# A local-attention, gated-convolution and MLP kernel: another hand-written list for its first fifth

## The chip, the cores and the metric

The kernel runs as one program on one core of a Trainium2 chip. The core has five engines that run their own instruction queues side by side: TensorE (PE, with its weight loads as PEld), VectorE (DVE), ScalarE (ACT), GpSimd (POOL) and SyncE (SP), which here only issues DMA transfers. The metric is the device time of one execution in microseconds (us), and lower is better.

## The reference

Three layers follow each other, in float32, on a batch of 2, 768 positions, 8 heads of 64:

```python
# 1 attention: each query sees its 31 nearest keys and 24 block summaries
k_sum = k.reshape(B, H, 24, 32, D).max(axis=3)
v_sum = v.reshape(B, H, 24, 32, D).mean(axis=3)
scores_l = where(|i - j| < 16, scale * q @ k.T, -1e9)
scores_s = scale * q @ k_sum.T + log(32)
a = softmax(concat(scores_l, scores_s))
x = a @ concat(v, v_sum)                 # -> (2, 768, 512)
# 2 gated convolution
h = relu(x @ w_in)                       # 512 -> 1024
x = (h * sigmoid(conv3(h, conv_w))) @ w_out
# 3 normalised MLP
x = x + relu(layernorm(x) * g_ln @ w_ch1) @ w_ch2    # 512 -> 2048 -> 512
```

The weights come as 64-bit floats, so the kernel itself narrows them to 32-bit ones, and each factor is split into a high and a low part, so that three fast products make one precise one.

## The kernel before

The kernel describes its work as 1932 numbered pieces (`plan.op`). A piece has a name, the engines that can do it, the pieces that it comes after, and the ring of buffers that it takes a place in. The string `ORDER` lists all of them: `13S 12S 15S` means that piece 13 is traced first, on SP, then 12, then 15. `plan.arrange` reads the list, and each engine's queue holds its own pieces in exactly this order. Nothing is reordered later: an engine that meets a piece whose input is not there stands until it is, and everything behind it in that queue stands too. The same holds for SP: a transfer that has to wait keeps back all transfers listed behind it.

The pieces of the first fifth, with the names used below:

- **Key and query loads** (`lk`, `lq`, L347): six key halves and four query halves of batch 0, 256 KB each, beside three value loads of 512 KB (`lvp`, for the block means). All transfers are on SP's queue.
- **Transposes** of keys and queries (L374): a group of 16 matmuls per half, into PSUM. Each key half is then copied out (`kn`, L265 or L267) and its blocks' maxima are taken (`kmb`, L395, on DVE).
- **The weights** (`lw`, L681 for w_in and L684 for w_out): sixteen loads of 512 KB. Each is narrowed by a DVE piece (L643), an ACT piece (L647) and a DVE piece (L652), then split into a high part (L265 or L267) and a low part (L664, POOL). Six loads have a place; the seventh waits until the first has been split.
- **Pairs** of score tiles. A pair is 128 queries by 8 heads. Its pieces are the mask product M (L479), the scores S (L487, 32 rows of the trace), per half the maximum X (L545, DVE), exponential E (L557, ACT), the sum's reciprocal Q and R, the scaling N (L576), the transpose P (L586) and its copy C; then T (L503), the product of both halves with the values, and the outputs H (high, L265 or L267) and L (low, L529, DVE). T of pair *j* needs two things in its value tile `vw`: the value rows (`lv`, L621) and the 24 rows of block means (`vs`), which `f_vs` puts there either by a DVE copy (L636) or by a DMA on SP (L634).
- **Two warm-up pieces** (L290): `warm0` with ten and `warm` with six products of a zeroed tile with itself, whose result is never read.
- **The convolution layer**: `h` (L741, 12 products in three pieces), then the taps, tanh and gate, and `x` (L818). The first piece of `h`, called h0 below, needs the attention output of pairs 0 to 2: it waits for the halo piece `xh1`, which waits for L of pair 2.

From the end of this first fifth (piece x110, an L818 group that starts at 97.6 us) both lists are the same to the end.

Of the kernel before, what the change touches and what calls it, by code (L numbers as in the profile page):

```python
# [8 lines left out]
115S 187S 57A 210P 197P 240P 239P 241P 214S 228G 104V 229V 88V 89A 211A 111A 198A 230V 215V 221V 165V 222V 110V 242V
231P 183P 2P 212P 249V 406S 243A 97S 250A 223G 244G 224P 188V 112V 106V 245V 251G 90G 116V 246V 232A 185A 247P 117A  # L10
225A 213V 186V 252V 206P 253V 107A 233P 118V 49A 248A 235A 207V 108G 413P 412P 414P 208V 96G 119A 113A 121S 236V 377S
254P 407P 409P 422V 237G 423A 259P 114G 120G 260P 261P 272P 273P 274P 262A 424G 263G 408V 410V 415V 416A 275A 123A 98V
255V 425V 264V 426V 265V 122V 285P 286P 127S 386S 411S 238S 133S 287P 298P 427P 276A 417G 99A 288A 289A 266A 428A 277V
278V 124V 437P 436P 299P 290V 100V 300P 311P 312P 438P 378P 313P 267V 268G 129A 279A 291V 301A 101A 292A 302A 125A
418V 280V 314A 269G 128V 439V 324P 270P 381P 271P 325P 102G 446V 681S 126G 303V 379V 315A 447A 440A 380V 293V 419V
304V 130V 369S 139S 316V 305A 281A 131A 135A 326P 327A 382A 282V 337P 338P 339P 350P 351P 352P 420P 421A 294G 448G
430G 441G 132G 317V 134V 295V 306V 383V 442V 136V 283P 256P 328A 353A 257A 354A 318A 449V 329V 330V 319V 429P 387P
137A 258V 138G 434G 284P 682P 388A 431A 307A 340A 389V 432V 433G 390P 373P 296P 297P 456P 457P 370P 458P 683A 331A
374A 341A 308V 355V 140V 450V 342V 356V 332V 141A 320A 459A 343V 344A 357A 321V 443V 142V 371A 391A 358V 372V 151S
145S 469P 309P 470P 153A 310P 471P 472A 482P 392V 375V 143G 144G 460V 483P 451P 484P 495P 496P 435S 147A 676A 473A  # L20
345V 485A 486A 677A 474V 461V 157S 399S 395S 710S 475V 476A 462V 487V 322P 497P 444P 508P 323P 509P 510P 463A 152V
464V 477V 376V 146V 488V 452A 333A 334V 498A 404A 499A 445A 684P 148V 154V 690P 689P 685A 385V 453P 158V 511A 500V
159A 713P 489A 712P 160V 521P 346A 149A 522P 490V 400V 405A 523P 150G 161A 691P 524A 454A 714P 155A 501V 393S 699V
335P 512A 732S 156G 722V 700A 336P 347V 162G 534P 396V 502A 535P 359A 348P 360G 536P 503V 686G 349P 692V 537A 525G
361P 687S 513V 538A 465G 455V 547P 362A 397S 365P 514V 737S 466V 548P 526V 366A 478G 549P 701V 539V 515A 479G 467P
527V 468P 707G 702V 516V 480P 491A 550A 492V 481P 528A 540V 394V 493P 504A 693A 494P 505G 566P 517G 529V 567P 703V
733P 694V 568P 367V 398V 506P 569A 551A 507P 541A 723A 579P 552V 530G 580P 695V 542V 581P 518V 724G 715V 704P 531G
582A 739P 734A 570V 740P 592P 705A 696V 519P 716A 725V 571V 401V 520P 572V 553V 593P 402A 543G 384V 583A 532P 403S
726G 554A 544V 680A 533P 594P 584V 741P 717V 555V 718V 595A 556G 697P 573A 749V 557G 727P 742V 750A 596G 545P 574V
585V 546P 719V 743A 558P 698V 688S 605P 738S 606P 728A 711S 744G 575G 607P 678G 720P 608A 679G 562P 559A 751G 609G  # L30
586A 735P 576G 761P 610V 706P 736A 563A 587V 760P 721V 618P 759S 588G 752V 619P 745V 753V 762P 597V 904P 770V 620P
598V 577P 621A 611V 560A 771A 622G 631P 708V 589G 632P 709V 633P 599A 772V 578P 600V 763V 754P 634A 601G 612A 905P
623V 729P 764A 773V 746V 624V 906P 774V 625A 730A 747P 907V 755A 590P 602V 908A 731V 644P 635V 645P 626V 591P 765V
613V 914V 646P 614G 766V 636V 603P 647A 748V 775P 767V 604P 776A 637V 915A 657P 627G 658P 659P 768P 660A 778G 628G
926P 638A 756P 769A 639V 561A 909V 910V 927P 777P 757V 911G 758V 928P 779A 615V 916V 917V 912P 929V 616P 648V 930A
780V 617P 649V 781G 629P 650V 661A 640G 936V 630P 651A 931G 662V 937A 782P 564V 663V 932V 783P 641V 933G 913A 784P
796P 785A 642P 786V 652V 797P 653A 664A 654V 798P 938V 939V 787V 810P 799A 788V 811P 800G 665V 789A 812P 924G 940V
# [1424 lines left out]
```

## Time and profile before

| | us |
|---|---|
| median of 3 runs | 473.87 (473.40 to 473.89) |
| the profiled execution | 473.54 |
| its span, first to last instruction | 471.8 |
| PE busy | 461.9 (98%) |
| DVE busy | 352.2 (75%) |
| ACT busy | 249.4 (53%) |
| POOL busy | 142.1 (30%) |

About 1.7 us of the execution lie outside the span. A busy PE is not the whole story: matmuls overlap, and where they run at half the clock they are counted as busy too. DMA is saturated at first (80% and more in the first five of 40 slices) and mostly idle later.

### The profile page before, as it was taken

What the parts mean: (1) busy time and instruction counts of PE and PEld (TensorE: products, weight loads), DVE (VectorE), ACT (ScalarE), POOL (GpSimd) and SP (SyncE); (2) the same over time, 40 slices, a digit from 0 to 9 for tenths busy, and PEclk for the clock granted to TensorE, in tenths of its full rate; (3) what the DMA queues carried; (4) which work ended last, traced back from release to release, by engine and by line L of the source; (5) the groups of instructions that cost most, each with busy time, mean ns of one, the idle gap of its engine ahead of it and who ended that gap; (6) DMA issues with size and microseconds to landing.
All of it is one profiled execution on the core that took longest, in us unless ns stands there. A gap on an engine that the chain in (4) does not pass through costs nothing.

```text
span 471.8 us, 8644 instructions
## 1 busy us (share of the span) xinstructions
PE 461.9 (98%) x3211; PEld 408.6 (87%) x3211; DVE 352.2 (75%) x705; ACT 249.4 (53%) x654; POOL 142.1 (30%) x185
## 2 busy tenths in 40 slices
PE   5999999999999999999999999999999999999996
PEld 5758999888899989988889899999898898998985
DVE  2899999996777857988998874677655677654643
ACT  2788989676766766968954432232343235322010
POOL 3547432554234244232523222131131332002000
PEclk9999999999999999999999999999999999999999
DMA  8999966902002202002221141202222022110213
GB/s 232 327 251 229 246 203 155 176 3 64 1 18 47 92 2 89 1 0 89 92 86 54 39 134 50 86 16 74 89 90 89 3 89 81 44 54 1 99 36 133
DMA packets 56121, 43.26 MB, mean 92 GB/s; under 512 B 34404, under 2 KB 46976, under 8 KB 56080
## 3 DMA queue, kind: packets, MB, share of 16 engines
q1 hardware_dynamic: 55936, 42.65, 32.4%
q8 instruction: 25, 0.41, 0.4%
q14 instruction: 16, 0.13, 0.1%
q10 hardware_dynamic: 144, 0.07, 0.1%
HBM read 39.22 MB, written 3.15 MB: 90 GB/s over the span
## 4 chain that ended last, share of the span: by engine, by line
PE 92%; DVE 3%; DMA 2%; ACT 2%; issue 1%; SPq 0%; POOL 0%; ACTq 0%; DVEq 0%; POOLq 0%
PE acc L1366 26%; PE ch L1288 22%; PE x L818 12%; PE h L741 6%; PE tr L741 5%; PE ch L741 4%; PE tr L487 2%; PE tr L503 2%; PE h L818 2%; PE tr L586 2%; PE tr L367 1%; PE tr L479 1%; PE tr L374 1%; PE x L881 1%; PE x L374 1%; DMA early<-in_k_dram 1%
## 5 line engine op out<-in xcount | busy, mean ns | idle before, releaser
L1366 PE MATMUL acc<-w,cb 128*128 128x512 f32 x570 | 138.1, 390 | 0.0
L1366 PEld LDWEIGHTS acc<-w,cb 128*128 128x128 f32 x570 | 106.4, 188 | 18.4
L1288 PE MATMUL ch<-xb,w 128*128 128x384 f32 x384 | 75.6, 338 | 0.3 <-DVE u L1299 0.3
L1288 PEld LDWEIGHTS ch<-xb,w 128*128 128x128 f32 x384 | 67.8, 188 | 3.2 <-DVE u L1299 1.0
L1299 DVE TENSOR_TENSOR u<-ch,u 128x384 f32<-128x384 f32 x64 | 34.9, 552 | 30.5 <-PE ch L1288 29.8
L1288 PE MATMUL ch<-xt,w 128*128 128x384 f32 x288 | 57.0, 338 | 0.3 <-DVE u L1299 0.2
L771 DVE SCALAR_TENSOR_TENSOR c<-h,ccol,c 128x256 f32<-128x256 f32 (+1 forms) x80 | 48.4, 615 | 9.3 <-POOL c L269 4.9
L1288 PEld LDWEIGHTS ch<-xt,w 128*128 128x128 f32 x288 | 50.8, 188 | 2.8 <-DVE u L1299 1.1
L818 PE MATMUL x<-wo,ghi 128*128 128x512 f32 x160 | 51.1, 401 | 0.0
L1099 POOL TENSOR_TENSOR w<-raw,w 128x512 fp32r<-128x512 f32 (+1 forms) x16 | 20.5, 1283 | 81.9 <-ACT w L1166 75.0
L1308 ACT ACTIVATE cb<-p 128x384 fp32r<-128x384 f32 x32 | 16.5, 519 | 40.4 <-PE acc L1366 23.6
L557 ACT ACTIVATE prob<-tr,nm 128x120 f32<-128x120 f32 x96 | 33.2, 368 | 5.6 <-DVE nm L545 3.6
L647 ACT ACTIVATE raw<-raw 128x512 f32<-128x512 f32 x32 | 21.0, 672 | 26.8 <-DMA raw<-in_moe_w_ch_dram 26.8
L741 PE MATMUL h<-xT,wi 128*128 128x258 f32 x216 | 32.0, 289 | 0.0
L818 PE MATMUL x<-wo,glo 128*128 128x512 f32 x80 | 31.6, 395 | 0.0
L818 PEld LDWEIGHTS x<-wo,ghi 128*128 128x128 f32 x160 | 27.9, 189 | 3.3 <-ACT wo L265 0.2
L1308 ACT ACTIVATE cb<-u 128x384 fp32r<-128x384 f32 x32 | 16.1, 521 | 27.4 <-DVE u L1299 27.3
L741 PEld LDWEIGHTS h<-xT,wi 128*128 128x128 f32 x216 | 29.1, 190 | 1.7 <-ACT h L753 0.2
L741 PE MATMUL tr<-xT,wi 128*128 128x386 f32 (+1 forms) x168 | 29.3, 317 | 0.0
L741 PEld LDWEIGHTS tr<-xT,wi 128*128 128x128 f32 x168 | 26.7, 190 | 1.3 <-issue 0.4
L652 DVE SCALAR_TENSOR_TENSOR raw<-raw 128x512 uint32<-128x512 uint32 x32 | 22.9, 727 | 0.7 <-ACT raw L647 0.2
L786 DVE SCALAR_TENSOR_TENSOR gbuf<-c,h 128x256 f32<-128x256 f32 (+1 forms) x40 | 19.3, 487 | 5.2 <-ACT c L776 5.1
(192 smaller groups left out, 830.0 us busy)
## 6 DMA issues: line engine op xcount, KB each, us to landing
raw<-in_moe_w_ch_dram SPq DMA_DIRECT2D x32, 512.0 KB, 3.6
wst<-in_moe_w_out_dram SPq DMA_DIRECT2D x8, 512.0 KB, 4.8
vw<-in_v_dram SPq DMA_DIRECT2D x20, 192.0 KB, 4.6
wst<-in_moe_w_in_dram SPq DMA_DIRECT2D x5, 512.0 KB, 8.3
s_q<-in_q_dram SPq DMA_DIRECT2D x8, 256.0 KB
early<-in_k_dram SPq DMA_DIRECT2D x6, 256.0 KB, 5.0
x2a<-in_moe_w_in_dram SPq DMA_DIRECT2D x3, 512.0 KB
early<-in_v_dram SPq DMA_DIRECT2D x3, 512.0 KB
```

What stands on the lines that cost most here:

```text
L557: A.activation(out=pr[:, p, :], in_=sc[:, p * NK:(p + 1) * NK], func=AF.Exp, bias=nm[:, p:p + 1], scale=1.0, accum_out=sm[:, p:p + 1])
L647: A.activation(out=f, in_=f, func=AF.Prelu, scale=F64_SCALE, alpha=F64_SIGN)
L652: V.scalar_tensor_tensor(out=most, in0=most, scalar=3, in1=least, op0=ALU.logical_shift_left, op1=ALU.bitwise_or)
L741: T.matmul(live["h", i][:, 0:N + 2], w_[:, c, f * 128:(f + 1) * 128], x_[:, c, 0:N + 2], start=(k_ == 0 and c == 0), stop=(k_ == 2 and c = ...
L771: V.scalar_tensor_tensor(out=ct, in0=ht[:, kk:kk + N], scalar=ccol[:, kk * NF + f:kk * NF + f + 1], in1=ct, op0=ALU.mult, op1=ALU.add)
L786: V.scalar_tensor_tensor(out=gt, in0=ct, scalar=1.0, in1=ht, op0=ALU.add, op1=ALU.mult)
L818: T.matmul(x2ps[g, t], l[:, ts_], r[:, f, :], start=(f == 0 and j == 0), stop=(f == NF - 1 and j == 2))
L1099: lambda e: on[e].tensor_tensor(out=hi()[1], in0=from_(), in1=hi()[0].bitcast(F32), op=ALU.subtract),
L1288: T.matmul(bk[k], l[:, c, :], x_[:, c, :], start=j == 0 and c == 0, stop=j == 2 and c == 1)
L1299: lambda e: V.tensor_tensor(out=temp(to), in0=bk[k], in1=temp(x), op=ALU.add), after,
L1308: A.activation(out=half(0, r, y), in_=temp(src), func=AF.Relu)
L1366: T.matmul(acc[key], ct_[n][l][:, r, 128 * t:128 * t + 128], w2[s][k][:, r], start=first and j == 0, stop=done and j == 5)
```

## The change

Only the string `ORDER` differs; no piece is added, removed or rewritten, and 24 lines fewer hold the string, so a line of the program after has a number lower by 24 (L503 becomes L479). The first 563 pieces are listed in another order, and 56 of them on another engine. The list begins:

```diff
-13S 12S 15S 14S 67S 9S 8G 3G 4G 5G 6G 68V 58V 0V 31P 32A 59A 69A 16S 11S 18S 17S 20S 73S 91S 19S 21S 39P 27P 34P 41V
+3G 0V 7G 2P 16S 15S 13S 42P 39P 43A 40A 12S 31P 44V 4G 163G 6G 33V 14S 45G 27P 41V 28A 29V 5G 34P 36V 17S 11S 24P 32A 25A 35V 30V 18S 67S 52P 53A 69A 73S
```

What moves, by names: eight key and query halves lead SP's queue and the first weight comes ninth, where it was fifth; the six-product warm-up leads PE's queue, and the ten-product one moves from in front of the first block-mean product to a place behind the last of them; the maxima of keys lead DVE's queue; the three copies of the block means into `vw` (L636 on DVE) become transfers on SP (L634 before, L610 after); and the transposes of the fourth query chunk, which stood in front of h0, come behind it.

The first place is the start of DVE's queue. Before, `wst` is the first weight, `craw` the convolution's taps, `warm` the zeroed tile, and `ksum` the maxima of keys:

```order
L643 TENSOR_SCALAR wst<-wst 128x512
L643 TENSOR_SCALAR craw<-craw 24x128
L285 MEMSET warm 128x64
L395 TENSOR_REDUCE ksum<-tr 128x2x8 x2
L652 SCALAR_TENSOR_TENSOR wst<-wst 128x512
L652 SCALAR_TENSOR_TENSOR craw<-craw 24x128
L902 COPY crow<-craw 24x128
L395 TENSOR_REDUCE ksum<-x_179 128x2x8
```

The same place after:

```order
L261 MEMSET warm 128x64
L371 TENSOR_REDUCE ksum<-x_127 128x2x8
L371 TENSOR_REDUCE ksum<-tr 128x2x8 x2
L371 TENSOR_REDUCE ksum<-x_182 128x2x8
L371 TENSOR_REDUCE ksum<-x_199 128x2x8
L243 COPY kw_95<-x_199 128x8x64
L243 COPY kw_94<-kw_94 128x4x3x16 x2
L371 TENSOR_REDUCE ksum<-tr 128x2x8
L619 TENSOR_SCALAR wst<-wst 128x512
```

The maxima now stand in front of the first narrowing, and the taps' pieces are far behind.

The second place is SP's queue from the last w_in load that both lists have there (the eighth place of `wst`) to the last transfer that T of pair 2 needs. Before (`vw0` to `vw2` are the value tiles of pairs 0 to 2, `s_q` a later query chunk):

```order
L954 DMA s_q<-in_q_dram 128x8x64 x2
L681 DMA wst<-in_moe_w_in_dram 128x4x256
L621 DMA vw_99<-in_v_dram 80x8x64
L621 DMA vw_99<-in_v_dram 96x8x64
L684 DMA wst<-in_moe_w_out_dram 128x1024
L621 DMA vw_100<-in_v_dram 96x8x64 x2
L621 DMA vw_101<-in_v_dram 96x8x64 x2
```

After (`vsum` is the tile of block means):

```order
L657 DMA wst<-in_moe_w_in_dram 128x4x256
L597 DMA vw_99<-in_v_dram 80x8x64
L597 DMA vw_99<-in_v_dram 96x8x64
L597 DMA vw_100<-in_v_dram 96x8x64 x2
L930 DMA s_q<-in_q_dram 128x8x64 x2
L610 DMA vw_99<-vsum 24x2x512
L597 DMA vw_101<-in_v_dram 96x8x64 x2
L610 DMA vw_100<-vsum 24x2x512
L828 DMA crow<-in_moe_g_ln_dram 4x128
L660 DMA wst<-in_moe_w_out_dram 128x1024
L657 DMA x2a<-in_moe_w_in_dram 128x4x256
L660 DMA wst<-in_moe_w_out_dram 128x1024
L610 DMA vw_101<-vsum 24x2x512
```

The last row, the block means of pair 2, now stands behind three weight loads; before, the value rows of pair 2 stood behind one of them, and the means came by DVE. (`vw_99`, `vw_100` and `vw_101` are the tiles `vw0`, `vw1` and `vw2`.)

## Rows read from the trace of the kernel before

**Rows 1.** The page's busy line of PE, and what PE waited for.

```profile
PE 461.9 (98%) x3211; PEld 408.6 (87%) x3211; DVE 352.2 (75%) x705; ACT 249.4 (53%) x654; POOL 142.1 (30%) x185
PE tr L374 <- DMA early<-in_k_dram: 4.9, 2, 4.0
PE tr L586 <- DVE prob L576: 0.5, 1, 0.5
```

**Rows 2.** Stretches: length, busy of PE, PEld, DVE, ACT, POOL, clock, DMA share, GB/s.

```profile
4.00:12.30 8.30, 7.42 (x68) 7.02 (x70) 2.96 (x8) 2.05 (x4) 1.63 (x7) 1.00 1.05 281
17.80:34.57 16.77, 16.77 (x196) 9.01 (x195) 15.51 (x37) 14.17 (x59) 8.67 (x13) 1.00 1.05 283
34.57:43.92 9.35, 8.90 (x161) 7.11 (x161) 8.83 (x18) 8.49 (x29) 6.46 (x9) 1.00 1.07 210
43.92:98.28 54.36, 54.36 (x530) 49.23 (x529) 53.32 (x109) 45.04 (x138) 23.47 (x32) 1.00 0.79 186
98.28:471.80 373.52, 368.92 (x2180) 331.61 (x2178) 266.46 (x524) 174.86 (x420) 96.35 (x105) 1.00 0.18 58
```

**Rows 3.** Timeline of PE up to 23 us: start, length, instruction, idle before it.

```profile
3.98 1.98 PE L374 MATMUL tr<-ident,early 128*64 128x128 f32 x16 [3.98 <-DMA early<-in_k_dram]
6.84 1.98 PE L374 MATMUL tr<-ident,early 128*64 128x128 f32 x16 [0.88 <-DMA early<-in_k_dram]
8.60 3.63 PE L374 MATMUL x<-ident,early 128*64 128x128 f32 x32
12.01 2.07 PE L374 MATMUL tr<-ident,early 128*64 128x128 f32 x32
15.66 1.04 PE L374 MATMUL tr<-ident,early 128*64 128x128 f32 x16
16.54 1.31 PE L479 MATMUL tr<-mask_r,mask_l 67*64 67x480 bf16 x6
```

**Rows 4.** Timeline of DVE: its first instruction, and the first maximum of scores.

```profile
9.31 0.43 DVE L643 TENSOR_SCALAR wst<-wst 128x512 uint32<-128x512 uint32 x1 [9.31 <-DMA wst<-in_moe_w_in_dram]
...
18.86 0.66 DVE L545 TENSOR_REDUCE nm<-tr 128x4 f32<-128x480 f32 x1 [0.35 <-PE tr L487]
```

**Rows 5.** Timeline of all engines, 32 to 44 us, the pieces around T and h0.

```profile
32.30 0.68 DVE L636 COPY vw<-vsum 24x1024 f32<-24x1024 f32 x1
34.57 1.15 PE L503 MATMUL tr<-probT,vw 120*64 120x64 f32 x32
35.66 1.47 PE L290 MATMUL h<-warm 128*128 128x512 bf16 x6
36.96 0.60 PE L367 MATMUL tr<-ident,s_q 128*128 128x128 f32 x4
39.00 2.21 PE L503 MATMUL tr<-probT,vw 120*64 120x64 f32 x64
41.15 0.58 PE L479 MATMUL tr<-mask_r,mask_l 67*128 67x480 bf16 x2
41.27 0.59 ACT L265 CAST xT<-tr 128x512 fp32r<-128x512 f32 x1
41.52 1.29 DVE L529 TENSOR_TENSOR xT<-tr,xT 128x512 fp32r<-128x512 f32 x2
43.13 1.04 PE L367 MATMUL tr<-ident,s_q 128*128 128x128 f32 x8
43.26 0.34 POOL L267 CAST xT<-xT 128x8 fp32r<-128x8 f32 x2
43.92 1.69 PE L741 MATMUL h<-xT,wi 128*128 128x258 f32 x12
```

**Rows 6.** DMA moved up to 40.53 us, from 10 to 20 us, and from 34.57 to 40.53 us.

```profile
DMA packets 20150, 10.47 MB, mean 258 GB/s; under 512 B 8212, under 2 KB 20016, under 8 KB 20144
...
DMA packets 4657, 3.17 MB, mean 317 GB/s; under 512 B 130, under 2 KB 4656, under 8 KB 4656
...
DMA packets 4048, 1.06 MB, mean 178 GB/s; under 512 B 4040, under 2 KB 4040, under 8 KB 4046
```

More of the change, by code (lines that the diff above doesn't have):

```diff
@@ L9 @@
[L9 to L13, printed above, removed]
@@ L94 @@
[L94 to L95 removed]
+3G 0V 7G 2P 16S 15S 13S 42P 39P 43A 40A 12S 31P 44V 4G 163G 6G 33V 14S 45G 27P 41V 28A 29V 5G 34P 36V 17S 11S 24P 32A 25A 35V 30V 18S 67S 52P 53A 69A 73S
+21S 9S 79S 19S 26V 50P 47A 68V 190P 167P 51V 70V 8V 74V 46V 38G 48A 71A 75A 20S 166P 168P 72G 176V 177A 22S 169V 170A 103S 171G 189P 191P 76V 54P 199V 200A
+178V 179V 63P 64A 180V 181P 65P 192V 80V 193A 81A 105A 172V 201V 202V 173V 203V 37G 104V 55P 217P 106V 77G 58V 23S 82V 194V 174P 182V 66A 49A 216P 218P
@@ new lines @@
+107A 226V 59A 240P 91S 92V 204P 205V 195V 56P 83A 175A 93A 219V 227A 94V 196V 78G 85S 220A 109S 164S 187S 209S 228V 239P 241P 229V 57A 86V 108G 249V 87A
+88V 84G 197P 198V 95A 165S 184G 230G 221G 96G 222V 242V 214S 188S 250A 60V 110V 223V 1P 111A 231P 251G 10S 243A 115S 97S 244V 183P 185A 252V 89A 232A 121S
+215S 112V 224P 206P 234G 253G 225A 186V 212P 210P 254P 377S 207V 208V 211V 245V 213A 246V 113G 90G 255V 413P 114G 233P 235A 412P 117A 236V 414P 61P 247P
+237V 248A 259P 260P 261P 272P 116V 62V 118V 273P 274P 119A 262A 422V 423A 275A 285P 286P 120G 98V 287P 415V 416A 298P 299P 300P 417G 311P 263V 436P 312P
@@ new lines @@
+424V 288A 122V 313P 264V 425V 276V 265V 266A 99A 426V 427P 123A 301A 302A 267V 268G 277V 278V 100V 133S 269V 418V 289A 124V 437P 438P 279A 280V 101A 314A
+315A 446V 125A 447A 439V 378P 303V 290V 127S 316V 102G 128V 440A 441G 317V 291V 419V 379A 428V 281A 324P 325P 270P 326P 337P 271P 380V 338P 339P 318A 135A
+319V 420P 282V 350P 421A 292A 304V 134V 126G 351P 293V 442V 352P 129A 305A 130V 283P 327A 131A 294A 448V 306V 136V 132G 430G 411S 284P 238S 256P 429P 406S
+409P 257V 295V 407P 353A 328A 354A 137A 431A 449V 329V 258V 340A 432V 138G 381P 296P 382A 297P 386S 387P 139S 410A 390P 355V 433V 330V 456P 457P 408A 140V
@@ new lines @@
+145S 151S 341A 342V 356V 141A 331A 458P 469P 307A 369S 357A 391A 332V 308V 459A 460A 470P 471P 482P 483P 484P 358V 343V 495P 344A 496P 497P 309P 508P 509P
+142V 472A 388A 473A 320A 461V 462V 510P 345V 681S 143G 389V 485A 383V 486A 463A 676A 147A 146V 434G 464V 321V 474V 450V 392V 435S 310P 511A 487V 153A 144G
+322P 333A 475V 476A 488V 512G 521P 522P 513V 477V 443V 677A 489A 157S 523P 148V 498A 451P 490V 452A 682P 683A 524A 514V 334V 149A 525A 684P 685A 373P 374V
+375V 444P 370P 150G 499A 371V 445A 515A 372V 323P 385V 500V 152V 158V 516V 404A 534P 535P 536P 335P 336P 453P 690P 399S 159A 713P 501V 547P 548P 376G 689P
@@ new lines @@
+160V 549P 537A 454A 346A 347G 154V 712P 155A 359A 526V 156G 707G 161A 691P 732S 400V 714P 162G 455V 538A 502A 699V 700A 550A 395S 465G 527V 503V 733P 348P
+349P 360V 361P 362A 528A 396V 466G 566P 710S 397S 686G 701G 398V 365P 366A 405A 539V 567P 467P 478G 479G 468P 480P 481P 568P 491G 492G 504A 505G 493P 494P
+702V 692V 569A 693A 722V 529V 367V 540V 517G 393S 694G 394V 737S 687S 506P 703V 551A 507P 541A 723A 579P 552V 530G 580P 695V 542V 581P 518V 724G 715V 704P
+531G 582A 739P 734A 570V 740P 592P 705A 696V 519P 716A 725V 571V 401V 520P 572V 553V 593P 402A 543G 384V 583A 532P 403S 726G 554A 544V 680A 533P 594P 584V
@@ new lines @@
+741P 717V 555V 718V 595A 556G 697P 573A 749V 557G 727P 742V 750A 596G 545P 574V 585V 546P 719V 743A 558P 698V 688S 605P 738S 606P 728A 711S 744G 575G 607P
+678G 720P 608A 679G 562P 559A 751G 609G 586A 735P 576G 761P 610V 706P 736A 563A 587V 760P 721V 618P 759S 588G 752V 619P 745V 753V 762P 597V 904P 770V 620P
+598V 577P 621A 611V 560A 771A 622G 631P 708V 589G 632P 709V 633P 599A 772V 578P 600V 763V 754P 634A 601G 612A 905P 623V 729P 764A 773V 746V 624V 906P 774V
+625A 730A 747P 907V 755A 590P 602V 908A 731V 644P 635V 645P 626V 591P 765V 613V 914V 646P 614G 766V 636V 603P 647A 748V 775P 767V 604P 776A 637V 915A 657P
@@ new lines @@
+627G 658P 659P 768P 660A 778G 628G 926P 638A 756P 769A 639V 561A 909V 910V 927P 777P 757V 911G 758V 928P 779A 615V 916V 917V 912P 929V 616P 648V 930A 780V
+617P 649V 781G 629P 650V 661A 640G 936V 630P 651A 931G 662V 937A 782P 564V 663V 932V 783P 641V 933G 913A 784P 796P 785A 642P 786V 652V 797P 653A 664A 654V
+798P 938V 939V 787V 810P 799A 788V 811P 800G 665V 789A 812P 924G 940V 643P 813A 925S 824P 814A 666G 903S 667G 815V 655P 656P 790V 941P 918V 791A 825P 801V
+792G 668P 802V 826P 669A 838P 816V 827A 363V 803A 672P 828G 942A 839P 670A 829V 817A 364A 804V 934P 840P 830V 673A 805G 818V 852P 841A 831A 853P 842G 368A
@@ new lines @@
+854P 806G 843V 674A 671A 919P 866P 920A 844V 855A 867P 935A 921P 845A 565A 846V 943P 856V 675A 857V 793P 1067V 832V 1068G 922V 868P 923V 880P 869A 944A
+1069V 881P 858V 870G 945V 882P 871V 794P 883A 872V 795P 1073S 884V 873A 1078S 807P 885V 1095A 808P 886V 819A 946P 820V 809P 947P 1074V 1075A 833A 821P
+1076V 1096A 834V 948P 1079V 1080A 822P 887A 823P 859A 860V 960P 847A 874V 1077A 835P 1081V 836P 848V 1082A 888V 837P 949A 1083G 1097P 861A 849P 950A 862G
+961P 951V 1085G 850P 851P 1084G 1089A 962P 1093V 1086G 1098P 963A 952V 974P 1110A 863P 1087A 964V 1090A 975P 1104A 1094G 976P 875A 1088A 864P 977A 1091G
@@ new lines @@
+1099V 988P 978A 876G 1191S 1100V 989P 965V 865P 1101V 877P 1102V 889G 966V 1108A 878P 1092G 1105V 953A 879P 967A 954V 990P 1111A 1185S 890V 1002P 991A 955G
+1103V 1003P 968V 979V 891P 992V 895P 956V 980V 1004P 896A 1192V 1113P 892A 1016P 1106A 1112P 1005A 1107V 1017P 981A 993V 1119A 1018P 1006A 982V 1109V 1030P
+1114A 1019A 899P 994V 1020A 1115V 1031P 969A 1007V 900A 1032P 970G 1008V 1125A 957P 897A 995A 958P 1021V 1009A 996V 959P 1187A 1116V 1044P 1022V 983A 1118V
+1033A 971P 1117V 1121A 984V 1045P 1034A 1010V 1122G 1023A 1046P 1035V 901A 893A 972P 1047A 1193A 973P 1126V 1123A 985P 997G 986P 998V 1124V 987P 1128P
@@ L96 @@
+1911P 1920P 1924P 1921V 1918P 1925V 1926P 1919V 1917V 1930P 1923V 1928P 1927V 1931V 1929V
 """
```

118 lines of the change are left out of this document (32 added, 86 removed).

## The prediction

> **What bounds the kernel now.** I read the page's busy line first, then what PE waited for, then a table by stretches, then the timelines of the engines at the two places where the list moves work. PE is busy for 461.9 of 471.8 us, and its waits are small: 4.9 us at the very start for keys and 0.5 us once for a scaled probability [rows 1]. So the end is set by when PE gets through its queue, and a change of the first fifth is worth as much as it moves the moment at which PE reaches the common rest of the list. From 43.92 us (h0) to 98.28 us PE has no idle time at all, and behind that it is busy for 368.9 of 373.5 us [rows 2]. I therefore ask one question: when does h0 start, and how much PE work is left between it and the common rest?
>
> In front of h0 the stretches show three things side by side. DMA is full: its share is 1.05 from 4 to 34.57 us and 1.07 up to 43.92 [rows 2]. DVE is nearly full too, 15.5 of 16.8 us and 8.8 of 9.4 us [rows 2]. And PE is slow at first: a group of 16 transposes takes 1.7 us (32 of them from 8.60 to 12.01) and 0.88 us at the end of the same work (15.66 to 16.54), although the clock column says 1.00 in that stretch [rows 2, 3]. The matmul times are those of 1.2 GHz until 12 us and of 2.4 GHz afterwards, and they rise after PE has worked without a break since 6.84 us.
>
> **The change part by part.** *The start.* Before, PE reaches the first mask products at 16.54 us [rows 3], behind nine groups of transposes; after, behind eight, since one query group has moved back (0.88 us). The scores need eight halves of keys and queries. Before, one weight of 512 KB stood among them, which is 0.52 MB, or 1.65 us at 317 GB/s [rows 6]. DVE began at 9.31 us, because its first instruction waited for that weight [rows 4], and the maxima stood behind it; after, they run as the transposes finish. The six warm-up products lead and cost nothing there, because PE stood until 3.98 us anyway [rows 3]; they may also bring the full clock sooner, which I price between nothing and the 2.5 us that three groups lost (3 times 1.7 minus 0.88), and put in nothing extra, since the loads come no sooner than DMA brings them. Taken together the mask products come at 16.54 - 1.65 - 0.88, so 14.0 us; I take 13.8.
>
> *From there to h0, if nothing but PE counted.* Before, 27.4 us pass from 16.54 to 43.92 [rows 3, 5], and PE is idle for 0.5 of them. After, this part has lost the six warm-up products (35.66 to 36.96, 1.3 us), and two transposes that now come behind h0 (43.13 to 43.92, 0.8 us), and has gained the query group (0.88): 27.4 - 1.3 - 0.8 + 0.9 = 26.2 us. So h0 could start at 13.8 + 26.2 = 40.0 us, 3.9 earlier. The 0.8 us come back behind h0, so PE would reach the common rest 3.1 us earlier.
>
> *What stands against it: SP's queue.* T of pair 2 needs its tile of values. I add up what stands in the queue up to its last transfer, from the sizes in the program. Before: ten halves of 256 KB, eight weights and three value loads of 512 KB, one query chunk of 512 KB, 1120 KB of value rows, 26 KB of small ones: 9850 KB, 10.09 MB. By 40.53 us, in the middle of that T (which is the second half of the 64 products from 39.00), DMA had moved 10.47 MB [rows 5, 6]. So before, the transfers were there just in time, with some 0.4 MB of the next ones. After, the means of pair 2 are a transfer too, and two weight loads more stand in front of it: 2 times 512 KB and 3 times 96 KB more, 11162 KB or 11.43 MB. That is 0.96 MB beyond what had been moved at 40.53. At the rate of the weights (317 GB/s) it takes 3.0 us, at the mean rate so far (258 GB/s) 3.7 us [rows 6]: T of pair 2 starts at 43.5 to 44.2 us. From below: value rows and the query chunk, 1.67 MB in pieces of 256 bytes, at 178 GB/s [rows 6] are 9.4 us, and the other 9.76 MB at 317 GB/s are 30.8 us; with 2 us until data flows that is 42.2 us, if the queue never runs dry. I take 43.5, nearest to the measured sum, and keep 42.2 and 44.5.
>
> What the rows show here is a queue that is full and whose sum fits the moment of use. The Trainium skill ("DMA: Bandwidth & Descriptors", Queues, rings and completion order) says that each DMA engine consumes its descriptors in ring order; by that a small transfer cannot pass the weights listed ahead of it, which speaks against this list. If small transfers did pass, the time would be that of the first rival below.
>
> *From T of pair 2 to h0.* The second T begins at 40.0 us before (39.00 plus half of the 64 products) and h0 at 43.92, but two transposes and DVE's queue stretch that. After, the steps are T 1.15 us, its high part 0.59 on ACT, the low part 0.65 on DVE, the halo 0.34 (now on DVE; on POOL it took that), with three hand-overs of 0.1 to 0.15 as between 41.15 and 41.27 [rows 5]: 3.2 us. The pieces that PE has meanwhile (scores, one mask product, a transpose) fill this and cost nothing. So h0 starts at 43.5 + 3.2 = 46.7 us, 2.8 later than before.
>
> *The copies.* Three DVE copies of 0.68 us [rows 5] leave DVE, 2 us of an engine that was nearly full. This gains nothing where PE waits for a transfer. If the queue were no bound it would be part of the 3.1 us above.
>
> *Behind h0.* PE has all of its old work to x110 plus the two transposes: 54.4 + 0.8 us, if it never waits. ACT, DVE and POOL have the same work per step as before, and the weights come sooner, so I put in no wait; a slip of up to 1 us belongs in the range.
>
> *Sum.* 2.8 + 0.8 = 3.6 us later at the common rest, which is dense, so it arrives at the end: 471.8 + 3.6 = 475.4 us of span and 473.54 + 3.6 = 477.1 for that execution. The median of the runs is 0.33 higher: 473.87 + 3.6 = 477.5 us. With the ends of the transfers' sum (42.2 and 44.5) and the slip of 1 us it is 476.2 to 479.5.
>
> **The rivals.** *The queue is not the bound.* If the transfers of block means land by 37 us, h0 comes at 40.0 and the time is 473.87 - 3.1 = 470.8 us. For it: PE was hardly seen to wait for a value tile, and some engines of the queue were idle between 37 and 40 us, as the mean of 178 GB/s suggests. Against it: 11.43 MB by 37 us is 327 GB/s from 2 us on, more than even the weights alone reached [rows 6]. It decides if T of pair 2 starts before 40.7 us; this is the case on the other side, faster.
>
> *About as much won as lost.* The transfers come at some 40 to 41 us, h0 at about 43.2, and the 0.8 us behind it bring the time to within 0.9 us of before. For it: the two bounds lie on both sides. Against it: it needs the queue 1.5 to 2 us better than from below.
>
> *The clock falls.* After, PE has done its fifth probability transpose at about 32 us and then stands for the first value tile: 9.27 MB stand in front of it in the queue, which had 9.40 MB through at 34.57 before, so up to 36 us. In the trace of before PE has no such gap after 12 us. If the clock goes back to 1.2 GHz, it takes once more what the start took: 5.2 us at half the rate (6.84 to 12.01 [rows 3]), so 2.6 us, and the time is 480.1 us. The Trainium skill ("TensorE: Matmul & The Clock Gate", Why this matters for your kernels) warns of idle gaps between matmul bursts for this reason; no row here shows a gap that is long enough to tell. The ten warm-up products stand right in front of this gap and speak against it.
>
> *The list does not do what it says.* That the maxima move ahead but nothing is gained there, because ACT copies of the same tiles still come first, would shift the start by 1 us at most and disappear behind the queue: it changes neither sign nor forecast.
>
> **How the numbers follow.** Queue-bound without a fall of the clock: 0.52, 476.2 to 479.5 us, likeliest 477.5. Clock falls too: 0.14, about 480. Queue no bound: 0.22, about 470.8. Near zero: 0.12. About 0.2%, 0.95 us, is what a measurement of this kernel can tell from no change. Faster by more than that 0.22, within it 0.12, slower 0.66. The range from 471.0 to 480.3 leaves out half of the faster case and half of the clock's. The likeliest case has its own range, 476.2 to 479.5.
>
> **What would show it.** Right: in the profile after, T of pair 2 (L479 there) starts at 42 to 44.5 us and the wait ahead of it is ended by a transfer into `vw`, not by an engine; h0 (L717) starts at 46 to 48; PE's idle time between 30 and 47 us is several us, where it was 0.5; the mask products start at about 14 us; x111 starts at about 102 instead of 98.3. Wrong: T of pair 2 before 40 us; PE as dense as before between 20 and 45 us; or waits on DVE or ACT in front of T. Matmuls of doubled length behind 32 us would be the third rival.

## The result and the profile after

The changed kernel takes 478.19 us (median of 6 runs, 477.95 to 481.05) beside 473.86 us for the kernel before. The ratio is 1.0108, with a 95% interval of 1.0085 to 1.0131: slower by about 1.1%, as forecast (477.5). The profiled execution took 477.95 us, its span is 476.2 us (471.8 before). The median is close; the parts of the sum are less so.

The table by stretches of the kernel after, cut at the mask products, the fifth probability transpose, T of pair 0, T of pair 2, h0 and x111 (columns as in [rows 2]):

```profile
3.98:13.07 9.09, 8.54 (x128) 8.08 (x128) 4.96 (x10) 3.60 (x7) 2.61 (x12) 1.00 1.09 307
13.07:32.10 19.03, 18.27 (x211) 9.55 (x210) 18.05 (x42) 18.53 (x73) 9.53 (x12) 1.00 1.17 283
32.10:37.01 4.91, 0.52 (x5) 0.31 (x4) 2.66 (x8) 2.19 (x11) 2.65 (x4) 1.00 1.20 202
37.01:45.36 8.35, 5.97 (x82) 5.11 (x82) 4.02 (x7) 2.71 (x5) 2.56 (x2) 0.80 1.08 274
45.36:48.31 2.95, 2.95 (x71) 2.47 (x71) 1.10 (x4) 1.19 (x2) 0.00 (x0) 1.00 0.08 16
48.31:103.88 55.57, 55.57 (x539) 49.99 (x536) 53.18 (x112) 46.06 (x140) 23.35 (x31) 1.00 0.80 175
103.88:476.20 372.32, 368.34 (x2180) 331.62 (x2178) 265.94 (x525) 174.89 (x420) 97.19 (x106) 1.00 0.18 58
```

Between 32.10 and 45.36 us PE is busy for 6.5 of 13.3 us, and so are DVE (6.7) and ACT (4.9), while the DMA share stays above 1: no engine is busy for more than half of this time, and the queue works all through. From h0 on PE is as dense as before [rows 2]. PE's waits, where 4.9 us for keys and 0.5 us stood before [rows 1]:

```profile
PE tr L479 <- issue: 6.8, 2, 4.4
PE h L266 <- DVE warm L261: 1.0, 1, 1.0
PE tr L350 <- DMA early<-in_k_dram: 0.4, 1, 0.4
```

Two waits of T (L479) make 6.8 us. The profile names no releaser here ("issue"), but the completions that the trace keeps of each transfer do: the block means of pair 0 are complete at 36.92 us and T of pair 0 starts at 37.01; those of pair 2 at 45.27, and T of pair 2 starts at 45.36. PE's timeline of this place (start, length, instruction, idle before it) answers [rows 5]:

```profile
32.02 0.60 PE L562 MATMUL tr<-ident,prob 128*120 128x128 f32 x4
37.01 1.93 PE L479 MATMUL tr<-probT,vw 120*64 120x64 f32 x32 [4.39 <-issue]
38.87 1.11 PE L562 MATMUL tr<-ident,prob 128*120 128x128 f32 x4
39.91 1.41 PE L479 MATMUL tr<-probT,vw 120*64 120x64 f32 x32
41.25 1.09 PE L343 MATMUL tr<-ident,s_q 128*128 128x128 f32 x8
42.18 0.60 PE L562 MATMUL tr<-ident,prob 128*120 128x128 f32 x4
42.62 0.37 PE L455 MATMUL tr<-mask_r,mask_l 67*128 67x480 bf16 x1
45.36 1.15 PE L479 MATMUL tr<-probT,vw 120*64 120x64 f32 x32 [2.38 <-issue]
48.31 1.68 PE L717 MATMUL h<-xT,wi 128*128 128x258 f32 x12
```

T of pair 0 takes 1.93 us, T of pair 2 takes 1.15: behind the first gap the clock was at half. At the start the six warm-up products lead, and the full rate came early (compare [rows 3]):

```profile
1.04 2.74 PE L266 MATMUL h<-warm 128*128 128x512 bf16 x6 [1.04 <-DVE warm L261]
4.10 1.97 PE L350 MATMUL x<-ident,early 128*64 128x128 f32 x16 [0.31 <-DMA early<-in_k_dram]
5.83 2.20 PE L350 MATMUL tr<-ident,early 128*64 128x128 f32 x32
7.85 1.93 PE L350 MATMUL x<-ident,early 128*64 128x128 f32 x32
13.07 0.90 PE L455 MATMUL tr<-mask_r,mask_l 67*128 67x480 bf16 x5
```

Thirty-two transposes take 1.9 us from 7.85 us on (3.63 before), and the masks stand at 13.07 instead of 16.54 us. PE won 3.5 us at the start and had lost 4.4 by h0.

### The profile page after: what moved, and what is told of

It reads as the page before. It is cut to its first block, busy times and chain, and to the rows that moved or that the text cites. A ratio compares the mean times of both kernels' runs of the same rounds, so it can differ in the third digit from the quotient of the medians.

```text
span 476.2 us, 8631 instructions
## 1 busy us (share of the span) xinstructions
PE 462.9 (97%) x3211; PEld 407.9 (86%) x3211; DVE 350.0 (74%) x705; ACT 250.5 (53%) x656; POOL 140.9 (30%) x180
## 4 chain that ended last, share of the span: by engine, by line
PE 90%; DMA 2%; DVE 2%; SPq 2%; ACT 2%; issue 1%; DVEq 0%; ACTq 0%
PE acc L1342 27%; PE ch L1264 23%; PE x L794 12%; PE h L717 6%; PE tr L717 5%; PE ch L717 4%; PE tr L479 3%; PE h L794 2%; PE tr L562 2%; PE tr L463 2%; DMA early<-in_q_dram 1%; PE tr L343 1%; SPq L323 1%; PE acc L1205 1%; ACT prob L533 1%
## 5 line engine op out<-in xcount | busy, mean ns | idle before, releaser
L628 DVE SCALAR_TENSOR_TENSOR raw<-raw 128x512 uint32<-128x512 uint32 x32 | 21.8, 694 | 0.7 <-ACT raw L623 0.2
```

What stands on the lines that cost most here:

```text
L628: V.scalar_tensor_tensor(out=most, in0=most, scalar=3, in1=least, op0=ALU.logical_shift_left, op1=ALU.bitwise_or)
```

## The experiments

All are compared with the kernel before on the same chip, where its median lay between 473.1 and 473.8 us. Every time below has its ratio with a 95% interval. The medians come from different chips, so two rows are best compared by their ratios. The places are starts in the profiled execution, in us:

| kernel | masks | T pair 0 | T pair 2 | h0 | x111 | time | ratio |
|---|---|---|---|---|---|---|---|
| before | 16.54 | 34.57 | 39.98 | 43.92 | 98.28 | 473.86 | 1 |
| after | 13.07 | 37.01 | 45.36 | 48.31 | 103.88 | 478.19 | 1.0108 |
| a_means_dve | 13.44 | 33.69 | 39.61 | 43.53 | 99.12 | 474.04 | 1.0019 |
| a_means2_ahead | 13.04 | 37.44 | 43.82 | 46.77 | 102.35 | 476.83 | 1.0080 |
| b_means2_late | 16.20 | 34.41 | 46.21 | 52.32 | 106.68 | 480.79 | 1.0155 |
| b_means2_warm | 16.36 | 34.75 | 46.62 | 50.47 | 104.83 | 479.03 | 1.0113 |
| a_warm_gap | 13.14 | 38.06 | 45.77 | 51.00 | 107.00 | 480.82 | 1.0156 |
| a_warm_gaps | 13.10 | 37.04 | 45.27 | 48.22 | 103.79 | 477.75 | 1.0086 |
| a_means_pool | 12.98 | 34.68 | 42.59 | 45.71 | 101.31 | 475.05 | 1.0034 |
| a_early | 12.64 | 34.71 | 39.56 | 42.79 | 103.06 | 476.27 | 1.0057 |
| b_start | 14.62 | 34.49 | 40.08 | 44.06 | 98.33 | 473.34 | 0.9989 |
| b_best | 14.45 | 34.44 | 39.19 | 43.03 | 99.85 | 474.81 | 1.0023 |
| b_tuned | 14.57 | 37.59 | 42.71 | 46.51 | 102.66 | 478.21 | 1.0078 |
| b_tuned1 | 15.32 | 34.51 | 39.72 | 43.53 | 99.64 | 475.12 | 1.0029 |

My theory was that the place of the block means in SP's queue sets T of pair 2 and with it the end. The rivals were the engines' order of work, and the clock.

### The means on DVE again

```diff
-... 165S ... 188S ... 215S ...
+... 165V ... 188V ... 215V ...
```

> The changed kernel with one part undone: the three copies of the block means are DVE pieces again, at the same places of the list. Queue theory: T of a pair then waits for its value rows alone; T of pair 0 starts at about 32.6 us (37.0 in the changed kernel), T of pair 2 at 38.5 to 39.5 (45.4), h0 at 41.7 to 42.7 (48.3), and the time is 478.2 - 6 = 472.2 us, between 471.4 and 473.4. Rival, the order of the engines' work: if the probabilities or DVE's queue make T late, T of pair 2 stays near 45 and the time at 478 to 480, since DVE has three copies of 0.7 us more.

Measured: 474.04 us, ratio 1.0019 (1.0006 to 1.0032), where 472.2 was expected. T of pair 2 came at 39.61, within 0.2 us of what the queue theory said: what the changed kernel lost is the three transfers. But h0 came at 43.53, a microsecond later than expected, and the masks' lead of 3.1 us over the kernel before had shrunk to 0.4. The waits of PE from 30 to 45 us in this run, the stretch from the masks to h0, and the part of it from T of pair 0 on:

```profile
PE tr L562 <- DVE sm L541: 1.5, 1, 1.5
PE tr L479 <- issue: 0.7, 1, 0.7
PE h L717 <- DVE xT L243: 0.7, 1, 0.7
...
13.44:43.53 30.09, 26.47 (x365) 16.12 (x363) 28.96 (x63) 25.31 (x91) 15.14 (x17) 1.00 1.08 271
...
33.69:43.53 9.84, 7.67 (x151) 6.27 (x151) 9.70 (x21) 5.89 (x16) 4.46 (x4) 1.00 0.98 264
```

DVE (third of the busy times) works 29.0 of 30.1 us, and 9.7 of the last 9.8. With the queue out of the way DVE is what is late next. This is read from the waits and the busy times; no run takes work off DVE and changes nothing else.

### One transfer moved, both ways

In the changed kernel the means of pair 2 move ahead of the three weights; in the kernel before, they alone become a transfer, listed behind a query chunk and a weight.

```diff
 after, SP:   ... 188S
+215S
 10S 115S 97S 121S
-215S
 377S ...
```

> The changed kernel, only the transfer of the block means of pair 2 moved in SP's queue from behind three weight loads to the place directly behind the means of pair 1. Queue theory: it lands at about 40 us (45.3 in the changed kernel); PE then reaches T of pair 2 after T of pair 1, two transposes, a probability transpose and a mask product, at about 42.9 us, h0 at 45.9, and the time is 478.2 - 2.4 = 475.8 us, between 475 and 476.6. Rival, the transfer itself: if a copy of 96 KB from one tile to another is slow wherever it stands, it lands at 44 us or later and the time stays at 477.5 to 478.5.

Measured: 476.83 us, ratio 1.0080 (1.0050 to 1.0111). The means were no longer waited for: T of pair 2 follows the mask product without a gap, and h0 comes 1.5 us earlier. That is less than the 2.4 us expected, since T of pair 0 waits as before, the clock falls there, and now the slow products behind it are bare (T of pair 1 takes 1.83 us). The place in the queue is confirmed, the size was too high.

```diff
 before:
-215V (DVE)
 ... 97S
+215S
 250A ...
```

> The kernel before, with one part of the change alone: the block means of pair 2 are a transfer on SP's queue, listed behind the next query chunk and one more weight load, where they were a copy on DVE. Queue theory: that weight landed at 44.05 us, so the means land at about 44.5, T of pair 2 starts at 44.6 (40.0 before), h0 at 47.8 (43.9), and the time is 473.9 + 3.9 = 477.8 us, between 477 and 478.6. Rival, small transfers are not held up by large ones listed ahead: the time stays at 473.9, or falls to 473.2 because DVE has one copy less.

Measured: 480.79 us, ratio 1.0155 (1.0126 to 1.0185). One small transfer, behind a query chunk and a weight of 512 KB each, costs more than the whole change. PE's waits from 30 to 60 us, and the stretches around T of pair 2:

```profile
PE tr L503 <- DMA vw<-vsum: 6.1, 1, 6.1
...
39.01:46.21 7.20, 1.15 (x33) 1.03 (x33) 3.15 (x6) 2.07 (x5) 3.81 (x3) 0.88 0.97 256
46.21:52.32 6.11, 6.11 (x79) 4.91 (x79) 1.51 (x3) 2.29 (x6) 2.66 (x4) 0.59 0.31 66
```

Here the profile names the transfer as the releaser. Two things were larger than I expected: T of pair 2 starts at 46.2 instead of 44.6, and from there to h0 it takes 6.1 us instead of 3.9 before [rows 5], with a granted clock of 0.59.

### The clock

```diff
 b_means2_late
+1932P (27 zeroed products, unread) 
 233P (T of pair 2)
```

> The kernel before with the late transfer of the block means of pair 2, as in the run b_means2_late, and a third warm-up piece of 27 products (about 5.8 us, read by nothing) in PE's queue directly in front of T of pair 2, where PE stood for 6.1 us. Clock theory: PE ran at half its clock from that gap on, T of pair 2 to h0 took 6.1 us; now the clock stays at 1.00, T of pair 2 starts at 46.2 as in that run, h0 at 49.5 instead of 52.3, and the time is 480.8 - 2.8 = 478.0 us. Rival, the 6.1 us are waits for other engines: h0 stays at 52 and the time at 480.8.

Measured: 479.03 us, ratio 1.0113 (1.0090 to 1.0136). The stretch that took 6.11 us:

```profile
46.62:50.47 3.85, 3.85 (x79) 3.23 (x79) 1.50 (x3) 2.13 (x6) 1.17 (x3) 1.00 0.55 118
```

The same 79 matmuls take 3.85 us at a granted clock of 1.00. So 2.3 us of that profiled execution's loss was the clock, which had fallen behind the gap; the rest is the wait. h0 came at 50.5 and not at 49.5, since this stretch holds 3.9 us of PE's own work in this list, which I had put at 3.3.

```diff
 after:
 231P (probability transpose)
+1932P (20 zeroed products, unread) 
 183P (T of pair 0)
```

> The changed kernel with a third warm-up piece of 20 products (about 4.3 us) in the gap of PE before T of pair 0; its result is read by nothing. Queue theory: the clock then stays at 1.00 between 37.1 and 40.5 us and T of pair 0 takes 1.15 us instead of 1.9, but T of pair 2 still starts at 45.3, when the block means land, and the time is 478.2 us, within 0.4. Clock theory: the fall of the clock is itself part of the loss, and the time is 1.3 to 2.6 us shorter, 475.6 to 476.9.

Measured: 480.82 us, ratio 1.0156 (1.0125 to 1.0187). Neither theory had this: filling the gap made the kernel slower. T of pair 0 ran at the full clock (1.15 us), but the products before the wait for pair 2 were then done 0.4 us sooner, the means came 0.4 us later, PE stood 3.23 us there instead of 2.38, and the clock fell at the worst place:

```profile
45.77 1.98 PE L479 MATMUL tr<-probT,vw 120*64 120x64 f32 x32 [3.23 <-issue]
...
45.77:51.00 5.23, 5.22 (x71) 4.34 (x71) 1.93 (x6) 1.16 (x2) 0.00 (x0) 0.50 0.08 16
```

From T of pair 2 to h0 it took 5.23 us at half the clock, 2.95 in the changed kernel. With both gaps filled:

```diff
 after:
 231P
+1932P (15 zeroed products)
 183P ... 413P
+1933P (13 zeroed products)
 233P
```

> The changed kernel with both gaps of PE filled: a piece of 15 products (3.2 us) in front of T of pair 0 and one of 13 (2.8 us) in front of T of pair 2; read by nothing. With the first gap alone filled, the clock fell in the second, directly in front of T of pair 2, and the time was 480.8 us. Clock theory: with both filled the clock is 1.00 throughout, T of pair 2 starts at 45.4 to 45.8, h0 at 48.5 to 49, and the time is 478.0 to 478.6 us, as in the changed kernel, where the half clock lay ahead of the wait for the means and cost nothing. Rival, warm-up products in this place cost time themselves: 480 us or more.

Measured: 477.75 us, ratio 1.0086 (1.0059 to 1.0113), h0 at 48.22: the changed kernel's time without any fall of the clock. So in the profiled execution of the changed kernel the fall cost nothing, because PE had to wait for the means of pair 2 anyway. Its other executions have no trace: two of the six took 480.23 and 481.05 us, the latter at a mean granted clock of 0.985 (0.996 in the profiled one), while all four of a_warm_gaps, at 0.999 and 1.000, lay between 477.43 and 478.15. There the fall may have cost up to 3 us; this is not shown.

### Where the early start went

```diff
-... 165S ... 188S ... 215S ...   (("S", 60), ("V", 602))
+... 165G ... 188G ... 215G ...   (("S", 60), ("V", 602), ("G", 800))
```

> The changed kernel with the three copies of the block means on POOL, at the same places of the list. With them on DVE the queue was no bound any more, but DVE was busy for 29.9 of the 31 us up to h0 and h0 came at 43.5. If DVE's load was what kept h0 there: T of pair 0 at 33 to 34.5 us, T of pair 2 at 38.5 to 39.5, h0 at 41.8 to 42.8, and the time is 472.4 to 473.4 us, 1.5 to 0.5 below before. Rival: POOL's copies hold up POOL's scalings and slow DVE beside them, h0 stays at 43.5 or later and the time at 474 to 475.

Measured: 475.05 us, ratio 1.0034 (1.0023 to 1.0045), a little behind the copies on DVE: the rival. DVE and POOL at one place of this run:

```profile
29.37 0.68 DVE L628 SCALAR_TENSOR_TENSOR x2a<-x2a 128x512 uint32<-128x512 uint32 x1
...
38.01 2.46 DVE L628 SCALAR_TENSOR_TENSOR wst<-wst 128x512 uint32<-128x512 uint32 x1
...
37.94 1.03 POOL L612 COPY vw<-vsum 24x1024 f32<-24x1024 f32 x1
38.94 0.98 POOL L552 TENSOR_TENSOR prob<-prob,sm 128x480 f32<-128x480 f32 x1
```

The same DVE instruction takes 0.68 us at 29.37, where POOL is idle, and 2.46 us at 38.01, where it ends half a microsecond after POOL's second instruction. Work moved to POOL came back as longer work on DVE. PE then paid a second time: it waited for DVE in front of the probability transpose of pair 1, and behind that gap its clock was at half.

```profile
37.90 1.08 PE L562 MATMUL tr<-ident,prob 128*120 128x128 f32 x4 [2.07 <-DVE sm L541]
...
38.91:40.80 1.89, 1.89 (x33) 1.79 (x32) 1.89 (x2) 0.59 (x1) 1.27 (x3) 0.50 1.08 354
```

T of pair 1 (38.91 us, 32 products) took 1.98 us instead of 1.15.

```diff
 after, SP:
-109S 164S 187S 209S 165S 214S 188S 10S 115S ... 215S
+10S 164S 187S 165S 188S 214S 215S 209S 109S 115S ...
 (w_in 7 narrowed behind xh1; 212P 210P behind 233P; 414P behind 261P)
```

> The changed kernel with its means as transfers, but with the large transfers that T does not need moved behind them on SP's queue: the value rows and the means of pairs 0 to 2 stand directly behind each other, and the query chunk and the load of the eighth weight (with its narrowing) follow; PE's transposes of that query chunk come behind T of pair 2, and the scores of one tile behind the first piece of h. Queue theory: 2 weights and a query chunk fewer stand in front of the last means (1.5 MB, 4.8 us), T of pair 0 starts at 33 to 34, T of pair 2 at 37.5 to 39 (45.4), h0 at 41 to 42 (48.3), and the time is 471.5 to 473 us, below the kernel before. Rival, the engines' work is then the bound as with the means on DVE: h0 at 43.5 and 474 us.

Measured: 476.27 us, ratio 1.0057 (1.0039 to 1.0076). In front, the queue theory nearly held: T of pair 2 came at 39.56 (37.5 to 39 expected), h0 at 42.79 (41 to 42). Behind h0 it was all given back: 60.3 us to x111, of which one unit of scores (1 us) had been moved there. PE's waits from 32 to 60 us, one row of ACT's timeline, and what PE did behind the longer wait:

```profile
PE h L717 <- ACT h L729: 1.7, 1, 1.7
PE tr L479 <- DMA vw<-vsum: 1.2, 1, 1.2
...
44.78 1.24 ACT L623 ACTIVATE wst<-wst 128x512 f32<-128x512 f32 x2 [2.51 <-DMA wst<-in_moe_w_out_dram]
...
48.83 2.79 PE L717 MATMUL h<-xT,wi 128*128 128x258 f32 x12 [1.72 <-ACT h L729]
51.41 2.08 PE L717 MATMUL tr<-xT,wi 128*128 128x258 f32 x12
...
48.83:51.30 2.47, 2.47 (x12) 2.47 (x13) 2.31 (x5) 2.47 (x16) 2.39 (x3) 0.54 0.30 54
```

The row of ACT: it stood 2.5 us for a w_out weight that now landed at 44.8 us, with the first step behind h in its queue after that. PE waited 1.7 us for that step, and behind the wait its clock was at half: 24 products of h took 4.5 us from 48.83 to 53.34, for which the changed kernel takes 2.9 (51.26 to 54.14). The scores, the wait and the clock make 4.3 of the 4.7 us that this stretch is longer than in the changed kernel. A load moved back needs its users moved back on every engine; I had moved those of one weight only.

```diff
 before:
+3G 0V 2P
 13S 12S 15S 14S
-67S 9S
 16S 11S 18S 17S 20S
+67S 9S
 ... (68V 58V 70V 60V, 69A 59A, 71G 72G behind the maxima and copies; 103S between 22S and 23S)
```

> The kernel before with the change's start alone: nine halves of keys and queries lead SP's queue and the first weight and the taps come behind them, the maxima of keys lead DVE's queue, the six-product warm-up leads PE's queue; the means stay copies on DVE, and the order of the later loads stays (only the second value load changes places with the seventh weight). If PE alone counted, the mask products come at 14.0 us (16.54 before), 1.3 us of warm-up are gone from the place behind T of pair 0, and the time is 473.3 - 3.8 = 469.5 us. Queue theory: the same bytes stand in front of the value rows of pair 2, which land at 40 to 40.5 us as before, so T of pair 2 cannot start before 40 and h0 comes at 43 to 43.6 (43.9): the time is 472.4 to 473.2 us. Rival, DVE (which has the first weight's narrowing behind the maxima now) is the bound: 473.3 us or more.

Measured: 473.34 us, ratio 0.9989 (0.9969 to 1.0009): no difference. The masks came 1.9 us earlier, h0 at 44.06 instead of 43.92. T of pair 2 started when the queue theory said, and PE's waits on the way name DVE:

```profile
PE tr L586 <- DVE prob L576: 1.9, 2, 1.4
...
14.62:44.06 29.44, 26.48 (x360) 16.08 (x355) 28.02 (x62) 24.74 (x92) 18.22 (x23) 1.00 1.10 261
```

DVE is busy for 28.0 of 29.4 us, 25.3 of 27.4 before. So PE is late at the probability transposes because of DVE. But the queue would have held T of pair 2 by itself: its two loads of value rows were complete at 39.95 and 40.62 us, and its two halves start at 40.08 and 40.67. Before, the last rows were complete at 40.49, and the second half started at 40.53. This run can't tell which of the two is worth more.

The last three versions are b_start with one more change each. The first moves two weight loads behind the value rows of pair 2, and their narrowing behind the halo piece:

```diff
 b_start, SP:
-109S 164S 115S 187S 214S
+164S 187S 214S 109S 115S   (110V to 113A, 114G and 116V to 119A, 120G behind 237G)
```

> The run b_start with the eighth w_in load and the first w_out load moved behind the value rows of pair 2 on SP's queue, and the narrowing of these two weights behind the halo piece on DVE, ACT and POOL. Queue theory: 1 MB (3 us) fewer stand in front of the value rows, T of pair 2 starts at 37.5 to 39 us (40.0 before), h0 at 41 to 42.3 (43.9), and the time is 1.6 to 2.9 us below before, 470.4 to 471.7 us. Rival, DVE is the bound over the whole first 98 us (53.3 of 54.4 us busy behind h0 before): the narrowing moved behind h0 gives back there what was won in front of it, and the time is 473 us.

Measured: 474.81 us, ratio 1.0023 (1.0007 to 1.0039). h0 came 0.9 us earlier than before and x111 1.6 us later:

```profile
43.03:99.85 56.82, 54.88 (x531) 49.25 (x529) 55.84 (x112) 46.63 (x141) 25.01 (x32) 1.00 0.76 179
```

The last value rows of pair 2 were now complete at 36.77 us, 3.7 earlier than before, and h0 won only 0.9: with the queue out of the way the engines' work was next. Behind h0 DVE is busy for 55.8 of 56.8 us. What it does not do in front of h0 it does behind it, and PE waits 1.9 us in all. The second (b_tuned) and the third (b_tuned1) put means on SP's queue ahead of the w_out load, whose narrowing moves behind the halo piece:

```diff
 b_start, SP:
-164S 115S 187S 214S ... (165V 188V 215V)
+164S 187S 165S 188S 214S 215S 115S   b_tuned
+164S 187S 214S 215S 115S ... (165V 188V)   b_tuned1
```

> The run b_start with the three means as transfers on SP's queue, but listed where the large loads do not stand in front of them: value rows of pairs 0 and 1, means of pairs 0 and 1, value rows of pair 2, means of pair 2, and only then the first w_out load, whose narrowing moves behind the halo piece. DVE theory (b_start lost its early start to DVE, 28.2 of 29.9 us busy): with 2 us of copies off DVE, the probability transposes in front of T of pair 1 no longer wait 1.4 us, T of pair 2 starts at 39 to 39.5 us (40.1 in b_start), h0 at 42.5 to 43.2 (44.1), and the time is 0.9 to 1.5 us below b_start, 471.8 to 472.5 us. Rival, the queue: the means are issued at 32 us at the earliest, when the block means are there, and land 3 to 5 us later behind what is queued; T of pair 0 waits until 36 or 37, the gap costs what DVE saves, and the time is 473.3 us or more.

> The run b_start with the means of pair 2 alone as a transfer, directly behind the value rows of pair 2 and in front of the first w_out load, whose narrowing moves behind the halo piece; the means of pairs 0 and 1 stay on DVE. Queue theory: the rows land 1.5 us earlier than in b_start, the means about 1 us behind them, T of pair 2 at 39.5 to 40, DVE has 0.7 us of copies and 1.1 us of narrowing less in front of h0, h0 at 43.2 to 43.6, and the time is 472.6 to 473.3 us. Rival, what is moved behind h0 is given back there: 473.5 us or more.

Measured: 478.21 us, ratio 1.0078 (1.0051 to 1.0106), and 475.12 us, ratio 1.0029 (1.0019 to 1.0040); each time it was the rival that came. In b_tuned the means were issued at 32.6 us, as soon as there were any, and were complete at 37.5, behind what was queued:

```profile
PE tr L503 <- DMA vw<-vsum: 3.1, 1, 3.1
```

In b_tuned1 h0 came 0.4 us earlier than before and x111 1.4 later.

No version beat the kernel before by more than its interval.

## Why the prediction was right, and where it was off

**The start.** Forecast 13.8, measured 13.07 us. The full rate, for which I had put in nothing, came early. What it is worth can be read from b_start and b_tuned1, whose lists are the same up to the masks (one execution each):

```profile
6.58 1.09 PE L374 MATMUL tr<-ident,early 128*64 128x128 f32 x16 [0.86 <-DMA early<-in_k_dram]
...
6.44 1.98 PE L374 MATMUL tr<-ident,early 128*64 128x128 f32 x16 [0.53 <-DMA early<-in_k_dram]
```

In b_start (first row) the second group already ran at the full rate, in b_tuned1 at half, and the masks came at 14.62 and 15.32 us: 0.7 us, as much as the forecast was off. Both lead with the six warm-up products, so these alone don't settle when the rate rises.

**T of pair 2, the main term.** Forecast 43.5 (42.2 to 44.5), measured 45.36: outside the bounds. The mechanism was right, as the two runs that moved one transfer show. The step that failed is the sum of bytes. I took 11.43 MB listed up to the last means, subtracted the 10.47 MB *moved* by 40.53 us before, and called 0.96 MB the rest. But only 10.09 MB were listed up to the last value rows, which were complete at 40.49: of the 10.47 MB, 0.07 were instruction loads on other queues, and 0.31 were already of transfers listed later. The same holds after:

```profile
DMA packets 21759, 12.00 MB, mean 265 GB/s; under 512 B 9037, under 2 KB 21353, under 8 KB 21753
```

When the means of pair 2 were there (stretch up to 45.36 us), 12.00 MB had moved, 0.57 more than stood in front (0.07 of it instruction loads). Listed against listed, the rest is 11.43 - 10.09 = 1.34 MB, and at the 258 to 317 GB/s that I used it takes 4.2 to 5.2 us from 40.5, where the last value rows were complete before: 44.7 to 45.7.

**From T of pair 2 to h0.** Forecast 3.2, measured 2.95 us. h0 at 48.31 instead of 46.7 is the miss of the step above, less 0.25.

**Behind h0.** Forecast 54.4 + 0.8, measured 55.57 to x111, 0.4 more, and the same in the five traces with this list and no wait behind h0 (55.57 to 55.61). I did not trace the 0.4.

**From x111 to the end.** I let the delay pass through undiminished. x111 was 5.6 us late, the end 4.4. The last stretch took 372.3 us (373.5 before [rows 2]); up to PE's first instruction of the third layer (L1205 after, L1229 before) both take 73.7 us, so the difference lies behind that. Over all fourteen traces the last stretch, the same list in each, took 372.3 to 373.8 us with no order by lateness. I count it as scatter; what makes it stays open. It covered 1.2 of the 2 us by which x111 came later than forecast, and that was luck.

**The copies.** I wrote that taking them off DVE gains nothing where PE waits for a transfer. That held, but the reverse mattered more: in a_means_dve, with the copies back and no transfer of means to wait for, DVE was the next bound.

**The rivals.** "The queue is not the bound" would have given 470.8 us. Its price was wrong as well as its condition: with the queue out of the way the time is 474.04, because I had asked only what PE needs up to h0, and DVE, "nearly full" in [rows 2], has as much to do and less slack. "About as much won as lost" needed the transfers at 40 to 41 us; the last was complete at 45.27. That nothing is gained at the start is answered by the masks at 13.07. "The clock falls" did happen, in the gap from 32 to 37 us, in spite of the ten warm-up products in front of it:

```profile
37.01:40.52 3.51, 3.51 (x48) 3.05 (x50) 0.69 (x1) 1.54 (x4) 0.33 (x1) 0.51 1.06 295
40.52:42.98 2.46, 2.46 (x39) 2.02 (x36) 1.57 (x3) 1.17 (x3) 2.23 (x2) 1.00 1.10 325
42.98:45.36 2.38, 0.01 (x2) 0.03 (x1) 1.75 (x4) 0.00 (x0) 0.00 (x0) 1.00 1.10 191
```

Its price of 2.6 us was about right where it is paid (2.3 in T of pair 2 to h0, b_means2_late against b_means2_warm), but in the profiled execution it lay in front of a longer wait and was not paid.

## What to carry to other kernels

A transfer on a queue that is full costs its place in the queue and not its size: three transfers of 96 KB held back a kernel of 478 us by 4 us (after against a_means_dve), the last of them, behind three weights, by 1.4 us alone (a_means2_ahead), and copies of 0.7 us on a busy engine were cheaper. When you sum a queue, set listed bytes against listed bytes at a known landing, and before you credit an earlier start, add up each engine's work up to the next meeting point: here, with the value rows 3.7 us sooner, the engines let h0 come only 0.9 us sooner (b_best). And ask of an idle gap not only what it lasts but what runs behind it, since the clock that falls there is paid by whatever comes next.

## What the runs showed of the hardware that was not expected

- The parts of one transfer on a full queue end at different times. Of the thirteen completions of the last means (issued at 37.32 us) twelve came between 43.23 and 45.27; the first came at 38.59, 1.3 us after the issue, and the other two transfers of means have such an early one too (1.7 and 1.3 us), so it seems to say nothing of the data. 0.50 MB of later transfers had moved by the last completion, 0.31 MB at the like point before. The Trainium skill ("DMA: Bandwidth & Descriptors", Queues, rings and completion order) has a ring of its own for each queue and engine; that completions spread over 2 us agrees.
- PE's granted clock fell to half at idle gaps of 6.1 us (b_means2_late), 4.4 us (after), 3.2 us (a_warm_gap) and 3.1 us (b_tuned), but also at gaps of 2.1 us (a_means_pool) and 1.7 us (a_early), and it stayed at 1.00 behind the gap of 2.4 us in front of T of pair 2 (after). So the length of a gap alone does not tell whether the clock falls. Filling only the first of two gaps cost 2.6 us against the changed kernel (2.3 by the ratios), since the fall came at the second.
- A DVE instruction with two inputs in SBUF took 2.46 us beside POOL's copy and product, 0.68 us alone. The Trainium skill ("SBUF — State Buffer", SBUF: two separate sides) calls the port pair of DVE and POOL an exclusive lock on which the loser fully blocks; the rows of a_means_pool agree: POOL's two instructions end at 39.92 us, and DVE's ends 0.55 us later.
